# Five instruction lists of a fused attention and gated-MLP kernel, written anew

## The chip, the cores and the metric

The kernel runs on one core of a Trainium2 chip. The metric is the device time of one execution in microseconds. The core has five engines that each work through a list of instructions of their own, in order: TensorE (matmuls, here PE or "pe"), VectorE (DVE, "dve"), ScalarE (ACT, "act"), GpSimd (POOL, "pool") and SyncE (SP, "sp"), which here issues loads and stores. They meet at semaphores only. An instruction that waits holds up everything behind it on its engine.

## The reference

One block of a network on 2048 tokens of width 448: local attention with a residual, then a gated MLP that mixes over tokens, with a residual.

```python
# A: 16 heads of 28; a token attends to 8 keys, 2 apart, ending at itself
qkv = layernorm(x) @ wqkv                       # 448 -> 3 * 448
attn = softmax(where(mask, q . k[pos - 2*w] * 28**-0.5, -1e9))   # w = 0..7
h = x + (attn @ v) @ wo
# B: Fh = 896
z = gelu_tanh(layernorm(h) @ w_in)              # 448 -> 1792
z1, z2 = z[..., :896], layernorm(z[..., 896:])
g = w_sp @ z2 + b_sp[:, None]                   # 2048 x 2048 over tokens
h2 = h + (z1 * g) @ w_out                       # 896 -> 448
```

Inputs and output are bf16.

## The kernel before

The program is cut into 677 tasks. A task is a named piece of work, from one DMA to 56 TensorE instructions, with the tasks that it depends on and the buffers that it takes and gives back (`Task`, L196). Which engine runs which tasks, in which order, is written out in one constant: `SEQ` (L35) holds five tuples of task numbers, for SP, POOL, DVE, ACT and PE. `Planner.replay` (L300) goes through the five tuples, at each step issues the task that could start first by its table of costs, and picks buffers on the way: PSUM as pairs of its eight banks, two slots for exponentials (`E`), two for reciprocals (`L`), three for values (`V`), four for transposed tiles (`tr`), three for sums (`ub`). Copies, some small functions and some DMAs may run on either of two engines (`alts`); the tuple in which the number stands decides. Its costs include one for TensorE's instructions: blocks of `CHUNK, ASK, NEED = 256, 118, 434` (L243), read as 256 instructions a block, asked for at instruction 118 and needed at 434 of the count. ScalarE's functions lie in two tables, one with exp and ln, one with gelu; a load (L508) is put in wherever the list goes from one to the other.

The tokens are cut into 16 blocks of 128. Block u and block u + 8 form unit u (0 to 7); units are worked from 7 down to 0. The names, with the lines that record them:

- `x*` (L553), `w*` (L566), `wo*` (L936), `win*` (L588): loads. `wsp0_b` and `wsp1_b` (L946) load block b of the mixing matrix transposed, lower and upper half; each waits for the one before it. `w_out` (L1044) may go when all attention is over, and `wsp1_7`, first of its half, waits on SP until w_out has landed.
- `bn1`, `rs1`, `nrm1` and `bn2`, `rs2`, `nrm2` (L656, L657, L646, L676): the first and second layernorm. The result is transposed into `xh` by TensorE and a copy (`tT`, L692; `ev1`, L641 on ScalarE, L643 on VectorE) or by a DMA from SP (`tD`, L683).
- `cp*` (L641, L643): copies of the weights into the layout of the matmuls (k, q, v; `cpw` for w_in).
- `mmk`, `mmq` (L783), `mmv` (L823) with the copies `evk`, `evq`, `evv` (L641, L643): the projections, in four chunks of the tokens.
- Nine attention tiles i of 114 tokens of each half: `mml` (L858) logits, `exp` (L870), `mask` (L877), `mmr` (L886) row sums, `ln` (L899), `rex` (L921), `mmo` (L911) weighted values, `ot` (L929) their product with the reciprocal.
- `mmy` (L964) and `h` (L972): output projection and residual of a unit; mmy of a unit needs all tiles that reach it.
- `mmz2` (L984), `ge` (L994), `bn3` (L1000), `ag3`, `rs3`, `nrm3` (L1014): second half of the MLP's first product ("second MLP product"), its gelu and layernorm. `mmz1` (L1028), `gz1` (L1038): the first half.
- `g` (L1064): mixing over tokens, with `ua`, `um` (L1073, L1081). `wo` (L1093), `oa` (L1103), `st` (L1108): last product, residual, store.

Each engine's tasks carry waits only where a dependency crosses engines. A wait for an earlier DMA that a task carries is a wait of the engine that issues it. The waits, the buffers and the order of the engines are thus all consequences of `SEQ`.

Of the kernel before, what the change touches and what calls it, by code (L numbers as in the profile page):

```python
# [35 lines left out]
    (5, 1, 4, 8, 11, 19, 13, 3, 12, 16, 300, 306, 10, 15, 17, 18, 297, 302, 14, 21, 296, 58, 20, 299, 76, 298, 70, 82, 64,  # L36
     310, 301, 311, 312, 307, 313, 314, 315, 305, 316, 333, 387, 369, 317, 351, 318, 319, 423, 405, 320, 498, 321, 441, 322,
     459, 500, 323, 501, 502, 324, 503, 325, 504, 505, 506, 507, 508, 499, 509, 510, 511, 512, 513, 514, 515, 596, 593, 626,
     566, 632, 629, 569, 563, 599, 602, 560, 635, 660, 664, 668, 672, 676),
    (28, 31, 26, 24, 29, 27, 25, 55, 87, 48, 85, 73, 86, 330, 384, 366, 348, 402, 420, 438, 341, 456, 395, 359, 413, 467,  # L40
     431, 377, 449),
    (23, 30, 40, 32, 33, 39, 35, 93, 36, 42, 94, 43, 38, 100, 54, 90, 91, 53, 88, 47, 99, 46, 56, 71, 57, 96, 49, 78, 50, 72,
     52, 65, 74, 75, 66, 77, 59, 68, 80, 69, 60, 81, 121, 62, 168, 63, 151, 125, 142, 176, 159, 303, 131, 139, 304, 83, 202,
     185, 210, 327, 193, 329, 328, 219, 345, 347, 236, 331, 227, 363, 332, 253, 381, 244, 382, 383, 364, 270, 385, 399, 386,
     261, 365, 287, 346, 367, 368, 417, 418, 278, 349, 295, 350, 401, 400, 309, 435, 419, 436, 421, 422, 403, 453, 455, 437,
     404, 454, 336, 339, 390, 375, 439, 440, 340, 393, 357, 457, 458, 394, 429, 372, 408, 354, 342, 426, 411, 376, 462, 465,
     412, 466, 358, 447, 444, 360, 430, 361, 396, 448, 343, 433, 378, 414, 397, 469, 468, 415, 451, 379, 432, 450, 583, 584,
     556, 574, 575, 580, 577, 557, 581, 571, 550, 572, 578, 586, 551, 589, 547, 590, 587, 553, 613, 614, 554, 607, 643, 608,
     604, 644, 548, 524, 622, 605, 619, 620, 534, 525, 595, 544, 535, 616, 545, 623, 592, 617, 610, 649, 611, 640, 625, 650,
# [1114 lines left out]
```

## Time and profile before

| | us |
|---|---|
| median of three runs (lowest, highest) | 242.42 (241.69, 245.83) |
| profiled execution | 242.73 |
| its span from first to last instruction | 240.9 |
| TensorE busy | 233.1 |
| VectorE busy | 140.3 |
| ScalarE busy | 96.1 |
| GpSimd busy | 26.9 |

Three stages can be told apart in the trace. Up to about 9.7 us loads and the first normalisation; then projections, attention, and the MLP's first product, in which three engines work side by side; from 120.5 us on the mixing product and the last product, in which VectorE adds and multiplies and stores leave at the end. Rows of the chain read: start, microseconds, what. Rows of the waits read: who waited, for whom, microseconds in total, times, longest. "issue" means that nothing in the profile shows what was waited for. In the groups: line, engine, operation, shapes, count, busy microseconds, mean nanoseconds of one, idle time before it.

### The profile page before, as it was taken

The page shows a single profiled execution, that of the slowest core. Times are in us where ns is not written, and L with a number is a line of the kernel's source. Part 1 is how long each engine was busy: PE and PEld are TensorE (multiplying, and loading weights), DVE is VectorE, ACT ScalarE, POOL GpSimd, SP SyncE. Part 2 cuts the span into 40 slices and gives each one's busy share as a digit, 9 for nine tenths or more (in the row PEclk, how much of TensorE's full clock was granted, in tenths as well). Part 3 has the DMA queues.
Part 4 walks back from the last instruction along what each step waited for, and adds up shares of the span by engine and source line. Part 5 has one row for each costly group of instructions (what it writes and reads, how often), then busy time and mean ns, then how long its engine had stood idle before and what let it go on. Part 6 is the DMA issues. An engine that isn't in the chain of part 4 may idle for free.

```text
span 240.9 us, 6695 instructions
## 1 busy us (share of the span) xinstructions
PE 233.1 (97%) x3009; PEld 119.9 (50%) x3019; DVE 140.3 (58%) x280; ACT 96.1 (40%) x113; POOL 26.9 (11%) x66
## 2 busy tenths in 40 slices
PE   7898999999999999999999999999999999999995
PEld 2486865456554544554444444444444444444453
DVE  5999959378999899788810050253101436554443
ACT  2996988889899947764730000000000000000000
POOL 4062000002014321304600000000000000000000
PEclk9999999999999999999999999999999999999999
DMA  7949575574213557987632733350000000010122
GB/s 213 337 106 103 112 125 95 97 127 53 44 22 77 109 85 174 169 133 117 141 76 58 174 68 65 85 46 0 0 0 3 0 0 19 20 60 0 38 93 78
DMA packets 54628, 20.01 MB, mean 83 GB/s; under 512 B 46792, under 2 KB 54472, under 8 KB 54600
## 3 DMA queue, kind: packets, MB, share of 16 engines
q1 hardware_dynamic: 53496, 18.67, 39.6%
q10 hardware_dynamic: 1104, 0.92, 1.3%
q8 instruction: 23, 0.38, 0.7%
q14 instruction: 5, 0.04, 0.1%
HBM read 6.37 MB, written 1.84 MB: 34 GB/s over the span
## 4 chain that ended last, share of the span: by engine, by line
PE 88%; DVE 5%; DMA 2%; issue 1%; POOL 1%; ACT 1%; SPq 0%
PE psum L1064 40%; PE psum L783 11%; PE psum L1093 9%; PE psum L984 8%; PE psum L964 5%; PE psum L823 5%; PE psum L1028 4%; PE psum L858 2%; PE psum L911 2%; DMA x_tm<-in_A_x_dram 2%; DVE z2p L1014 2%; PE psum L886 1%; DVE st L1000 1%; DVE tring L676 1%; POOL rs L647 1%
## 5 line engine op out<-in xcount | busy, mean ns | idle before, releaser
L1073 DVE TENSOR_TENSOR ub<-psum,reg 128x512 bf16<-128x512 f32 x28 | 18.9, 687 | 68.7 <-PE psum L1064 66.4
L1064 PE MATMUL psum<-reg,z2p 128*128 128x512 bf16 x220 | 49.4, 379 | 0.2
L1064 PE MATMUL psum<-wspT_lo,z2p 128*128 128x512 bf16 x218 | 48.5, 379 | 0.4 <-DVE z2p L1014 0.2
L1064 PEld LDWEIGHTS psum<-wspT_lo,z2p 128*128 128x128 bf16 x224 | 21.8, 98 | 26.6 <-issue 0.4
L1064 PEld LDWEIGHTS psum<-reg,z2p 128*128 128x128 bf16 x224 | 21.9, 98 | 26.2
L783 PE MATMUL psum<-xh,reg 64*128 64x128 bf16 (+2 forms) x448 | 26.0, 270 | 0.2
L1093 PE MATMUL psum<-reg 128*128 128x448 bf16 (+2 forms) x119 | 22.2, 341 | 0.1
L984 PE MATMUL psum<-w_in,xh 64*128 64x448 bf16 x224 | 22.2, 349 | 0.0
L1028 PE MATMUL psum<-xh,w_in 64*128 64x512 bf16 x196 | 21.8, 376 | 0.0
L641 ACT ACTIVATE reg<-psum 128x896 bf16<-128x896 f32 (+2 forms) x25 | 20.0, 844 | 1.9 <-PE psum L783 1.0
L783 PEld LDWEIGHTS psum<-xh,reg 64*128 64x128 bf16 x448 | 16.8, 94 | 7.8 <-issue 0.8
L656 DVE BATCH_NORM_STATS2 st<-x_tm 128x6 f32<-128x448 bf16 x32 | 19.6, 612 | 1.4 <-DMA x_tm<-in_A_x_dram 1.2
L1000 DVE BATCH_NORM_STATS2 st<-z2p 128x6 f32<-128x448 bf16 x32 | 17.5, 611 | 3.1 <-ACT z2p L994 3.1
L870 ACT ACTIVATE reg<-psum 128x928 bf16<-128x928 f32 x18 | 16.2, 939 | 4.1 <-PE psum L858 4.1
L646 POOL TENSOR_SCALAR rs<-mv 128x2 f32<-128x2 f32 x19 | 7.5, 393 | 88.4 <-DVE mv L657 70.2
L1038 ACT ACTIVATE reg<-psum 128x1024 bf16<-128x1024 f32 x14 | 13.6, 1029 | 8.0 <-PE psum L1028 8.0
L1093 PEld LDWEIGHTS psum<-reg 128*128 128x128 bf16 x119 | 11.4, 98 | 10.4
L994 ACT ACTIVATE z2p<-psum 128x896 bf16<-128x896 f32 x16 | 14.2, 916 | 5.6 <-PE psum L984 5.6
L1103 DVE TENSOR_TENSOR tring<-psum,x_tm 128x448 bf16<-128x448 f32 (+2 forms) x17 | 10.1, 596 | 10.2 <-PE psum L1093 10.1
L984 PEld LDWEIGHTS psum<-w_in,xh 64*128 64x128 bf16 x224 | 10.6, 94 | 10.4 <-issue 0.4
L929 DVE TENSOR_TENSOR reg<-psum,reg 128x912 bf16<-128x912 f32 x9 | 11.1, 1235 | 7.2 <-ACT reg L921 6.6
L1028 PEld LDWEIGHTS psum<-xh,w_in 64*128 64x128 bf16 x196 | 9.5, 94 | 11.5
(63 smaller groups left out, 205.9 us busy)
## 6 DMA issues: line engine op xcount, KB each, us to landing
x_tm<-in_A_x_dram SPq DMA_DIRECT2D x15, 112.0 KB, 4.2
out_dram<-tring SPq DMA_DIRECT2D x15, 112.0 KB, 1.7
w_in<-in_B_w_in_dram SPq DMA_DIRECT2D x2, 448.0 KB, 4.5
reg<-in_B_w_out_dram SPq DMA_DIRECT2D x1, 784.0 KB, 6.0
z2p<-in_A_wqkv_dram ACTq DMA_DIRECT2D x2, 336.0 KB, 4.5
reg<-in_B_b_sp_dram SPq DMA_DIRECT2D x1, 512.0 KB, 4.6
w_in<-in_B_w_in_dram SPq DMA_DIRECT2D x2, 224.0 KB, 4.3
reg<-in_A_wo_dram SPq DMA_DIRECT2D x4, 98.0 KB
```

What stands on the lines that cost most here:

```text
L641: iss("act", lambda e: e.activation(dst, src, AF.Copy), reads=rd, writes=wr)
L656: iss("dve", lambda e: e.bn_stats(st[:, b, :], x_tm[:, b, :]), reads=[r_x[b]], writes=[rl[b]])
L783: iss("pe", lambda e, c=c, s=s, gi=gi, lhs=lhs: e.matmul(psum[:, bk[s] * 512 + cw * gi:bk[s] * 512 + cw * gi + cw], lhs, xh[64 * s:64 * s ...
L870: iss("act", lambda e: e.activation(E[:, es[0], 2 * n:2 * n + 2, :], pair_view(lb, 0, 8 * JW), AF.Exp, scale=SCALE), reads=[r_bank[lb[0]], ...
L984: iss("pe", lambda e, k2=k2, c=BLK[s][k2], s=s: e.matmul(psum[:, zb[s] * 512:zb[s] * 512 + D], xh[64 * s:64 * s + 64, c, HX + 128 * u:HX + ...
L994: iss("act", lambda e: e.activation(z2p[:, u:u + 9:8, D * k:D * k + D], pair_view(zb, 0, D), AF.Gelu_apprx_tanh), reads=[r_bank[zb[0]], r_ ...
L1000: iss("dve", lambda e, b=b: e.bn_stats(st3[:, b, k, :], z2p[:, b, D * k:D * k + D]), reads=[r_z2[b][k]], writes=[r_st3[b][k]])
L1028: iss("pe", lambda e, k=k, c=BLK[s][k], s=s: e.matmul(psum[:, bk[s] * 512:bk[s] * 512 + 512], w_in[64 * s:64 * s + 64, k, 128 * f:128 * f ...
L1038: iss("act", lambda e: e.activation(z1p[f].rearrange("p (s t) -> p s t", s=2)[:, :, 512 * ch:512 * ch + 512], pair_view(bk, 0, 512), AF.Ge ...
L1064: iss("pe", lambda e, b=b: e.matmul(psum[:, gb[0] * 512:gb[0] * 512 + 512], z2p[:, b, 128 * f:128 * f + 128], src[:, b, 512 * (tc % 2):512 ...
L1073: iss("dve", lambda e: e.tensor_tensor(ub[:, us_[0], :], psum[:, gb[0] * 512:gb[0] * 512 + 512], bb[:, 512 * tc:512 * tc + 512], ALU.add), ...
L1093: iss("pe", lambda e, f=f: e.matmul(psum[:, wb[0] * 512 + d0:wb[0] * 512 + d1], z1p[f][:, 128 * m:128 * m + 128], w_out[:, f, d0:d1], star ...
```

## The change

Only `SEQ` changes: about 560 of the 677 positions hold another number. No task is added, taken away or resized, so TensorE has the same matmuls, and the table of costs stays.

- PE: the first projection is mmk3_2 (before: mmq3_0). mmv2, mmv1, mmv0 come later. The second MLP products of units 7 and 6 move up, to between the small products of tiles 4 to 2: "mmz2_7_0 mml2 mmy4 mmo3_0 mmo3_1 mmz2_7_1 mmz2_6_1 mmz2_6_0 mmo3_2 mmr2 mmo3_3 mmv1" (before, unit 7's stood among tiles 1 and 0, unit 6's behind all attention). The end of the attention reads "mmz2_5_1 mmr0 mmo0 mmo1 mmz2_5_0 mmz2_4_1 mmy0 mmy1 mmz2_4_0". The first groups of the mixing product stand in another order; from the thirteenth on all is as it was.
- ACT: "exp2_0 exp2_1 ge7_0 ge7_1 ge6_1 ge6_0 ln2 rex2 exp1_1 exp1_0 exp0_0 exp0_1 ln1 rex1 ln0 rex0 ge5_0" (before: "... exp0_0 exp0_1 ge7_1 rex1 ln0 rex0 ge7_0 ..."). gz1_1_0 comes last.
- Between DVE and ACT, work changes hands. To DVE: cpk001, cpq000, cpv1, cpw0_0, evk0_1, evk0_3, evk1_0, evv0, evv1. To ACT: cpk010, cpq001, cpq010, ev1_5, ev1_7, evk0_2, evk1_2, evq0_2, evq1_2. From ACT to POOL: rs1_0, rs1_3; the other way: rs1_1.
- DVE: cpw1_0, cpw0_1 and cpw0_0 stand between tiles 6 and 3, bn3_7_1 before ot2; the normalisations of units 7, 6 and 5 come earlier.
- SP: weights change queues (wq0, wq1, wv1 to SP; wk1, wv0 to ACT) and loads their order. In the second half: "wsp0_11 tD2_3 w_out wsp0_2 tD2_0 wsp1_7 tD2_2 tD2_1 wsp0_10" (before: "tD2_2 tD2_3 wsp0_2 w_out wsp0_10 tD2_1 wsp0_1 tD2_0 wsp1_7"). The last store, st15_1, leaves from ACT's queue.

The parts of the diff that hold the above, with the numbers (251 exp2_0, 335 ge7_0, 338 ge7_1, 356 ge6_1, 353 ge6_0, 255 ln2; 498 w_out, 500 wsp1_7, 423 tD2_2, 441 tD2_1, 459 tD2_0; 334, 337 mmz2_7, 355, 352 mmz2_6):

```diff
-    (5, 1, 4, 8, 11, 19, 13, 3, 12, 16, 300, 306, 10, 15, 17, 18, 297, 302, 14, 21, 296, 58, 20, 299, 76, 298, 70, 82, 64,
-     310, 301, 311, 312, 307, 313, 314, 315, 305, 316, 333, 387, 369, 317, 351, 318, 319, 423, 405, 320, 498, 321, 441, 322,
-     459, 500, 323, 501, 502, 324, 503, 325, 504, 505, 506, 507, 508, 499, 509, 510, 511, 512, 513, 514, 515, 596, 593, 626,
...
+    (4, 1, 5, 9, 6, 7, 11, 10, 12, 306, 19, 16, 302, 15, 17, 13, 21, 300, 18, 20, 297, 58, 296, 14, 76, 82, 70, 64, 298, 299,
+     301, 310, 311, 305, 312, 307, 313, 333, 314, 351, 315, 369, 316, 387, 317, 318, 319, 405, 498, 320, 459, 500, 423, 441,
+     321, 501, 322, 502, 323, 324, 503, 325, 504, 505, 506, 507, 499, 508, 509, 510, 511, 512, 513, 514, 515, 596, 593, 626,
...
-    (0, 6, 7, 9, 22, 2, 34, 95, 41, 92, 101, 45, 97, 89, 144, 107, 161, 115, 98, 105, 113, 103, 111, 109, 117, 166, 178, 67,
...
-     137, 133, 192, 217, 218, 212, 235, 234, 221, 226, 229, 251, 252, 238, 243, 255, 260, 268, 269, 263, 280, 272, 285, 286,
-     338, 277, 289, 294, 335, 389, 308, 371, 392, 374, 356, 353, 497, 485, 493, 491, 495, 410, 428, 407, 489, 425, 443, 461,
...
+    (0, 3, 2, 8, 22, 34, 41, 90, 38, 45, 98, 97, 105, 94, 103, 111, 93, 144, 95, 113, 161, 109, 52, 73, 107, 115, 117, 150,
...
+     187, 192, 137, 212, 234, 218, 217, 235, 246, 221, 226, 238, 229, 243, 251, 252, 335, 338, 356, 353, 255, 260, 269, 268,
+     285, 286, 272, 277, 289, 294, 371, 374, 389, 489, 392, 497, 410, 491, 487, 407, 464, 495, 461, 425, 428, 443, 475, 446,
...
-    (84, 37, 44, 106, 143, 160, 114, 104, 112, 110, 102, 108, 116, 51, 145, 146, 162, 147, 148, 163, 177, 122, 120, 164, 165,
...
-     266, 267, 262, 398, 271, 256, 257, 258, 259, 281, 282, 283, 284, 337, 416, 273, 274, 288, 275, 276, 334, 388, 290, 291,
-     292, 293, 434, 452, 373, 370, 391, 484, 352, 355, 496, 494, 492, 490, 409, 427, 406, 424, 488, 445, 442, 460, 463, 482,
...
+    (84, 37, 44, 104, 102, 110, 112, 143, 160, 51, 108, 106, 116, 114, 177, 145, 146, 147, 148, 124, 122, 118, 162, 163, 164,
...
+     181, 182, 326, 203, 138, 134, 186, 205, 188, 189, 190, 206, 207, 208, 191, 136, 211, 230, 231, 344, 213, 214, 215, 216,
+     245, 232, 233, 362, 220, 228, 237, 222, 223, 224, 225, 334, 247, 248, 249, 250, 380, 239, 240, 337, 355, 352, 241, 254,
+     242, 262, 256, 257, 258, 259, 264, 265, 266, 267, 398, 279, 281, 282, 283, 284, 416, 271, 373, 288, 290, 291, 292, 273,
+     274, 293, 275, 276, 370, 391, 452, 434, 388, 488, 494, 496, 409, 406, 490, 486, 463, 460, 427, 484, 424, 442, 445, 474,
...
```

34 rows, old and new, of the table SEQ are left out of this document.

## The prediction

> **What bounds the kernel now.** I read the page's busy times and its slices first.
>
> ```profile
> PE 233.1 (97%) x3009; PEld 119.9 (50%) x3019; DVE 140.3 (58%) x280; ACT 96.1 (40%) x113; POOL 26.9 (11%) x66
> PE   7898999999999999999999999999999999999995
> DVE  5999959378999899788810050253101436554443
> ACT  2996988889899947764730000000000000000000
> PEclk9999999999999999999999999999999999999999
> ```
>
> TensorE is busy in every slice after the start and has its full clock. VectorE and ScalarE come close to it only until about 120 us; in the second half (the token-mixing product and the output product) they mostly wait. A busy TensorE need not be a fast one, so next come its waits (microseconds, times, longest) behind the first product, and the chain in order of time (start, microseconds).
>
> ```profile
> PE psum L858 <- issue: 0.9, 1, 0.9
> PE psum L964 <- DVE mv L657: 0.8, 1, 0.8
> PE psum L823 <- issue: 0.3, 1, 0.3
> PE psum L1064 <- DVE z2p L1014: 0.2, 1, 0.2
> ```
>
> ```profile
> 5.92 0.64 DVE st L656
> ...
> 9.66 0.96 PE psum L783 x28
> ...
> 20.16 0.87 issue
> ...
> 52.35 0.26 issue
> ...
> 72.35 0.50 issue
> ...
> 120.50 10.72 PE psum L1064 x49
> ...
> 238.37 0.31 DVE tring L1103
> ```
>
> From 9.66 us, the first projection, to 238.3 us, the end of the last product, TensorE stands still for 0.9 + 0.8 + 0.3 + 0.2 = 2.2 us. The change reorders work and removes no matmul, so everything behind the start can yield 2.2 us at most. Of 242.42 us, 2% are 4.85 us, about what a measurement of this kernel can tell from no change. A gain of that size would need another 2.6 us from the 9.66 us of the start, where the first normalisation waits for loads until 5.92 us. So faster by over 2% is nearly excluded; the question is how much waiting the new order adds.
>
> **The change, part by part.** The sum is made against the profiled execution, 242.73 us (span 240.9), which lies 0.3 us above the median of the three runs, 242.42. I keep that distance.
>
> *The start.* The first product is now that of k, no longer of q. Rows of ScalarE's and VectorE's timelines (start, microseconds):
>
> ```profile
> 7.34 0.21 ACT L669 ACTIVATE rs<-rs 128x2 f32<-128x2 f32 x1
> 8.41 1.70 ACT L641 ACTIVATE reg<-reg 64x1792 bf16<-64x1792 bf16 x1
> 10.13 0.92 ACT L641 ACTIVATE xh<-psum 128x896 bf16<-128x896 bf16 x1
> 6.58 0.18 DVE L657 BATCH_NORM_AGGREGATE mv<-st 128x2 f32<-128x6 f32 x1
> 6.68 0.36 DVE L676 TENSOR_SCALAR tring<-x_tm,mv,rs 128x448 bf16<-128x448 bf16 x1
> 9.55 0.51 DVE L643 COPY reg<-reg 64x1344 bf16<-64x1344 bf16 x1
> 13.20 0.58 DVE L643 COPY reg<-z2p 64x1792 bf16<-64x1792 bf16 x1
> ```
>
> Four x tiles still come first, in another order, so the statistics end as now, at 6.76. On VectorE follow four normalisations and three k copies: 4 x 0.36 + 2 x 0.51 + 0.58 = 3.0, or 9.8 with gaps. On ScalarE stand the second unit's rstd (0.5, from 6.76), cpk010 (1.70, the row of that shape) and ev1_7, which moves there (0.92): 6.76 + 0.5 + 1.70 + 0.92 = 9.9. TensorE starts at about 10.05 in place of 9.66: **+0.4**. Bounds: -0.2 (VectorE as now) and +1.0 (the k weights, now issued first, land one copy later). Nothing hides this, since each later matmul waits behind the first. The weights that change between SP's and ScalarE's queues cost nothing further: ScalarE issues fewer of them ahead of its table load, and SP's next x load waits for x7 and x15 to land in either order.
>
> *TensorE's pauses.* Three of the rows above name no releaser.
>
> ```profile
> q8 instruction: 23, 0.38, 0.7%
> ```
>
> That queue carries 0.38 MB in 23 packets, 16.5 KB each; over the 6028 TensorE instructions of the page that is one packet per 262 instructions. The kernel's planner holds that a block of 256 is asked for at 118 and needed at 434 (CHUNK, ASK, NEED). Counted down the old list, two instructions a matmul, the pauses at 20.16, 52.35 and 72.1 stand at instructions 696, 2480 and 3756; 434 plus 1, 8 and 13 blocks is 690, 2482 and 3762. So I take them for late blocks. They come where the 316 instructions between asking and needing last only 4.5, 5.2 and 4.5 us by the rows; a stretch of 4.6 us had no pause. In the new list all stretches up to the attention's last tiles last 5.4 us or more, since value and second-MLP products stand between the small matmuls; three in a row late in the attention (before mml1_00, mml0_10 and mmo1_0) last 4.6, 4.3 and 4.65. So 0.87 + 0.26 + 0.75 = 1.9 go and I put back 1.2 for those three: **-0.7**. Bounds: -1.9 (none pauses) and +0.7 (all three pause by 0.87).
>
> [...]
>
> *Second MLP product and GELU among the exponentials.*
>
> ```profile
> L994 ACT ACTIVATE z2p<-psum 128x896 bf16<-128x896 f32 x16 | 14.2, 916 | 5.6 <-PE psum L984 5.6
> L508 ACT ACT_TABLE_LOAD x4 | 5.1, 1283 | 3.0 <-issue 2.9
> 96.14 5.30 PE psum L984 x56
> 30.83 2.77 PE psum L823 x56
> 34.47 3.13 PE psum L783 x28
> 78.72 3.13 PE psum L964 x16
> 78.80 1.23 DVE L929 TENSOR_TENSOR reg<-psum,reg 128x912 bf16<-128x912 f32 x1 [0.55 <-PE psum L911]
> L972 DVE TENSOR_TENSOR x_tm<-psum,x_tm 128x896 bf16<-128x896 f32 x8 | 8.7, 1086 | 2.5 <-PE psum L964 2.4
> L643 DVE COPY w_in<-w_in 64x3584 bf16<-64x3584 bf16 (+1 forms) x3 | 3.3, 1087 | 0.1
> L1000 DVE BATCH_NORM_STATS2 st<-z2p 128x6 f32<-128x448 bf16 x32 | 17.5, 611 | 3.1 <-ACT z2p L994 3.1
> ```
>
> Old and new both load tables four times. In the old order one gelu lies between two loads inside the attention (1.28 + 0.92 + 1.28 = 3.5), in the new one four (6.2). Behind them wait ln2, rex2, the last two tiles' exponentials, and so on VectorE ot2, ot1, ot0. Does TensorE feel it? The test is mmy0, which needs ot0. Today ot0 ends at 80.03 and the second product of the 78.72 row starts near 80.3: 0.2 us to spare. Between mmy7 and mmy0 the new list puts five second-MLP products (5 x 1.33), mmv2 (1.39), the last three q products (3 x 1.57) and mmr5, mmr6, mmo5 (1.2), and drops mmz2_4_0 and mmy1 (2.9): 13.9 - 2.9 = 11.0 us more. ScalarE between rex6 and rex0 gets three gelus (2.75), evv2 and evq0_1 (1.9) and loses evv1 and evv0 (1.8): 2.8 more. VectorE between h7 and ot0 gets three w_in copies (3.3), two value copies (2 x 1.09, by L972's size), ot5 (1.23), a pair of L1000 (1.2) and one normalisation (0.36): 8.2 more. So both keep their place, VectorE with 0.2 + 11.0 - 8.2 = 3.0 us to spare. The products of units 7 and 6 also want their transposed tiles sooner (unit 6 by 20.3 us of TensorE's list), and VectorE's list has moved the normalisations before them up by about as much (19.6), so those tiles keep their lead. What is left are single waits for a PSUM pair: mmz2_7_1 must wait until exp2_1 has freed one, mmr0 for its mask behind evv0, mmo1_0 for h2. I take **+0.6**; bounds 0 and +2.7 (the three gelus in full).
>
> *Before the mixing product.* Eight first-MLP products still follow the last second product, nrm3 has the same length, and the 0.2 before L1064 may go: **-0.15**, bounds -0.2 and +1.0 (the new third entry, g0_6_0, wants all of nrm3 0.4 us sooner). From there on the lists differ only in small swaps.
>
> *The last store.*
>
> ```profile
> 233.71 5.54 SPq L1108 DMA_DIRECT2D out_dram<-tring  x6
> ```
>
> SP issues stores until 239.25; the last sum, begun at 238.37, ends at 238.68. From ScalarE's empty queue the last store need not wait for the issue of the one before it: **-0.15**, bounds -0.4 and +0.1.
>
> Sum: 0.4 - 0.7 + 0.6 - 0.15 - 0.15 = 0.0. The profiled execution stays at 242.7, a median at **242.4 us**. [...]
>
> **The rivals.** *Slower: a load at the head of SP's queue.*
>
> ```profile
> 86.81 1.08 DVE L972 TENSOR_TENSOR x_tm<-psum,x_tm 128x896 bf16<-128x896 f32 x1
> 92.43 0.58 SPq L1044 DMA_DIRECT2D reg<-in_B_w_out_dram  x1
> 103.38 1.30 SPq L946 DMA_TRANSPOSE reg<-in_B_w_sp_dram  x1
> reg<-in_B_w_out_dram SPq DMA_DIRECT2D x1, 784.0 KB, 6.0
> DMA to landing us min/median/max: 2.9/3.0/6.2
> ```
>
> Now wsp1_7, which waits on SP until w_out has landed, is issued at 103.38, behind every transpose of unit tiles (L683). In the new list tD2_2 and tD2_1 stand behind it. w_out may go after the last h, now at 87.9 and by the list 1.6 later: 89.5. It lands 6.0 later, wsp1_7 takes 1.3, tD2_2 lands 2.9 to 6.2 after that (transposes into xh): 99.7 to 103.0. TensorE wants it for mmz2_2_1 near 101.4, the end of the four groups of the 96.14 row, which have as much matmul work before them. So 0 to 1.6 us are lost: within the forecast. But each further microsecond of w_out is one of the end. If it needs 11 us or more while transposes share the engines, the stall passes 5 us: **248 us**. Against it: 6.0 was measured with transposes around it. Chance 0.10. [...]
>
> *ScalarE becomes the bound of the attention's end.* Its slices there read 8 and 9; if the 3.0 us to spare are not there, the three gelus cost all of 2.7 in place of 0.6: 242.4 + 2.1 = 244.5. Chance 0.17.
>
> *All pauses go.* The three dense stretches pass, too, and the PSUM waits are nothing: 242.4 - 1.2 - 0.6 = 240.6. Chance 0.15.
>
> *Pauses do not follow the order:* they came from the transfers of the moment, the same 1.9 us stay, and 242.4 + 0.7 = 243.1. For it speaks that a block lands by DMA beside others, against it that all three stand at a block's end. Chance 0.08.
>
> **How the numbers follow.** The forecast has 0.50. Its own range, with half of the bounds, is 240.9 to 244.5. The range for 8 in 10 leaves out the slow rival and the far ends of the bounds: 242.4 - 2.2 = 240.2 (the start 0.6 below what I took, the pauses 1.2, the PSUM waits 0.4) and 242.4 + 3.9 = 246.3 (gelus +2.1, w_out's 1.6, 0.2 of the tail). Slower by over 2% (247.3): the slow rival's 0.10 and 0.02 for the gelus and the queue together, 0.12. Faster by over 2% (237.6): 0.02, for a start I misjudge. Within: 0.86.
>
> **What would show it.** First projection near 10.05 us. No pause over 0.2 us without a releaser before 65 us, up to three between 66 and 80 us. A ScalarE stretch of load, four gelus, load of 6.2 us, with TensorE's waits beside it below 1 us. tD2_2 issued right after wsp1_7 near 97 us. L1064 starting between 119.5 and 121.5, then 118 us to the end as now. The prediction is wrong if TensorE waits several microseconds for PSUM or VectorE between 60 and 100 us, or at mmz2_2_1.

## The result and the profile after

| | before | after |
|---|---|---|
| median, us (20 runs each) | 242.43 | 243.86 |
| lowest and highest | 241.23, 245.83 | 242.76, 245.59 |
| profiled execution | 242.73 | 242.96 |
| its span | 240.9 | 241.2 |

The ratio is 1.0067, with a 95% interval of 1.0045 to 1.009: the new order is slower by 0.7%, or by 1.4 us of the medians. The forecast was no change at 242.4, with a range of 240.2 to 246.3. The time lies in the range, but the forecast is missed by more than the measurement is uncertain.

The two profiled executions differ by 0.23 us only, so most of the difference is not in this trace. First, what is in it. These are TensorE's waits in the changed kernel (microseconds, times, longest), all of them:

```profile
PE psum L692 <- DVE tring L676: 2.1, 2, 1.1
PE psum L635 <- DVE warm L614: 1.5, 1, 1.5
PE psum L984 <- DVE x_tm L972: 0.5, 1, 0.5
PE psum L783 <- ACT reg L641: 0.5, 2, 0.3
PE psum L858 <- ACT reg L899: 0.3, 1, 0.3
```

No pause without a releaser is left: the old list had 0.9 and 0.3 of them and a third inside a wait of 0.8. New are the waits for the addition of L972, for the copies of L641 and for the logarithm of L899. The first row was, in the kernel before:

```profile
PE psum L692 <- DVE tring L676: 1.0, 2, 0.6
```

TensorE now stands idle for twice as long around the first two transposes. Its timeline there (start, busy, what, idle time before it) and VectorE's:

```profile
2.76 4.28 PE L635 MATMUL psum<-warm 128*128 128x512 bf16 x12
8.11 0.56 PE L692 MATMUL psum<-ident,tring 128*128 128x128 bf16 x7 [1.07 <-DVE tring L676]
9.69 0.56 PE L692 MATMUL psum<-ident,tring 128*128 128x128 bf16 x7 [1.02 <-DVE tring L676]
10.22 3.30 PE L783 MATMUL psum<-xh,reg 64*128 64x128 bf16 x112
```

```profile
6.79 0.85 DVE L643 COPY reg<-z2p 64x1344 bf16<-64x1344 bf16 x1
...
8.37 0.85 DVE L643 COPY reg<-z2p 64x1344 bf16<-64x1344 bf16 x1
```

The first projection starts at 10.32 us by the chain (rows of matmuls overlap a little, hence the 10.22) instead of 9.66. The two copies (cpk001 and cpk011) stand between the normalisations that the transposes wait for, at 0.85 us each. Before, two smaller copies stood there:

```profile
7.06 0.39 DVE L643 COPY reg<-z2p 64x672 bf16<-64x672 bf16 x1
8.18 0.39 DVE L643 COPY reg<-z2p 64x896 bf16<-64x896 bf16 x1
```

That is 2 x 0.46 = 0.92 us more. The last statistics ended 0.27 us sooner than in the trace of before (6.49 instead of 6.76), because their x tile had landed sooner, which leaves the 0.65 us.

From the first projection to the first mixing product, and from there to the last residual, busy times by engine (window, its length, busy time and instructions of PE, PEld, DVE, ACT and POOL, granted clock, two DMA figures), after and before:

```profile
10.32:120.74 110.42, 108.97 (x2423) 61.33 (x2422) 93.91 (x189) 86.90 (x102) 25.63 (x53) 1.00 0.62 110
120.74:238.85 118.11, 118.07 (x569) 55.15 (x567) 40.90 (x74) 1.94 (x2) 0.00 (x0) 1.00 0.18 43
```

```profile
9.66:120.49 110.83, 108.64 (x2424) 61.98 (x2426) 94.12 (x189) 89.12 (x105) 24.12 (x51) 1.00 0.62 111
120.49:238.37 117.88, 117.37 (x557) 55.02 (x565) 38.76 (x75) 1.82 (x2) 0.00 (x0) 1.00 0.19 43
```

The middle stage is shorter by 0.41 us: TensorE's idle time fell from 110.83 - 108.64 = 2.2 to 1.45, and its busy time grew by 0.3. The last stage is longer by 0.23. So this execution reads +0.66 at the start, -0.41, +0.23 and -0.2 at the last store: +0.3 of span.

What the trace doesn't show is in the list of executions. Of the 20 of the changed kernel, 9 have a mean granted clock of 0.986 to 0.993 and a median of 244.65 us; the other 11 have 0.999 or 1.0 and a median of 243.21. So the runs at a lower clock are 1.4 us longer. A stretch of 3.41 us at half clock, as e4_new_start's trace below has one (9.74 to 13.15 us, mean clock 0.993), lowers the mean by 0.007 and costs, as an estimate from its length, up to half of it, 1.7 us. Of the 106 executions of the kernel before that ran beside the experiments, 2 are below 0.999.

### The profile page after: what moved, and what is told of

It is laid out like the page before. It is cut to its first block, busy times and chain, and to the rows that moved or that the text cites. A ratio compares the mean times of both kernels' runs of the same rounds, so it can differ in the third digit from the quotient of the medians.

```text
span 241.2 us, 6695 instructions
## 1 busy us (share of the span) xinstructions
PE 233.8 (97%) x3019; PEld 119.3 (49%) x3019; DVE 143.2 (59%) x280; ACT 93.8 (39%) x111; POOL 28.4 (12%) x68
## 4 chain that ended last, share of the span: by engine, by line
PE 86%; ACT 5%; DVE 4%; DMA 1%; POOL 1%; issue 1%
PE psum L1064 40%; PE psum L783 9%; PE psum L1093 9%; PE psum L1028 9%; PE psum L984 9%; PE psum L964 5%; ACT reg L641 3%; PE psum L823 2%; PE psum L858 2%; DVE st L656 1%; ACT reg L899 1%; DMA x_tm<-in_A_x_dram 1%; PE psum L911 1%; DVE tring L676 1%; DVE x_tm L972 1%
## 5 line engine op out<-in xcount | busy, mean ns | idle before, releaser
L1064 PE MATMUL psum<-wspT_lo,z2p 128*128 128x512 bf16 x224 | 49.0, 379 | 0.0
L641 ACT ACTIVATE reg<-psum 128x1024 bf16<-128x1024 f32 (+2 forms) x24 | 19.3, 844 | 2.3 <-PE psum L783 1.9
L647 POOL TENSOR_TENSOR rs<-rs,nhalf 128x2 f32<-128x2 f32 x20 | 16.8, 842 | 1.7
L646 POOL TENSOR_SCALAR rs<-mv 128x2 f32<-128x2 f32 x20 | 6.4, 318 | 87.3 <-DVE mv L657 72.9
```

The costliest lines, as they stand in the source:

```text
L641: iss("act", lambda e: e.activation(dst, src, AF.Copy), reads=rd, writes=wr)
L647: iss("pool", lambda e: e.tensor_tensor(dst, dst, nh, ALU.pow), reads=rr + [r_nhalf], writes=rr)
L1064: iss("pe", lambda e, b=b: e.matmul(psum[:, gb[0] * 512:gb[0] * 512 + 512], z2p[:, b, 128 * f:128 * f + 128], src[:, b, 512 * (tc % 2):512 ...
```

## The experiments

Edits are given in the names of the tasks; "DVE", "PE" and so on are the tuples of SEQ. In the experiments' profiles the line numbers are higher by one or two. Ratios are to the kernel before, with 95% intervals.

**The start and the rest, put together crosswise.** In e3_old_start the new lists follow the old lists' start; in e4_new_start the old lists follow the new start.

```diff
 e3_old_start
-SP, POOL, DVE, ACT, PE: new lists
+SP up to x0, POOL to c_kpad, DVE to nrm1_13, ACT to evq2_2, PE to tT1_5: old lists
+then what is left of the new lists, in their order
 e4_new_start
-SP, POOL, DVE, ACT, PE: old lists
+SP up to x3, POOL to c_ones, DVE to cpq100, ACT to ev1_5, PE to mmq2_0: new lists
+then what is left of the old lists, in their order
```

> The new lists behind the old lists' start (loads, first normalisation of units 7 to 4, copies of the q, k and v weights, first projections up to the transpose of unit 5, with mmv6 behind tile 8's logits as before). Start theory: the first projection at 9.7 us, clock as in the kernel before, and the pauses that went stay gone: 241.3 to 242.2 us, at or below the kernel before. Attention theory: 243.5 to 244 us.

> The old lists behind the new lists' start, the mirror of the run before. Start theory: first projection at 10.3 us, a clock below 1.0 in part of the executions, and the old pauses: 243.3 to 244.3 us. Attention theory: as the kernel before, 242.4 us.

Measured: e3_old_start 245.2 (ratio 1.0094, 1.0061 to 1.0127), e4_new_start 245.6 (1.0124, 1.0086 to 1.0163). Both missed. A row of e3_old_start's timeline of TensorE (in brackets the idle time):

```profile
50.52 0.28 PE L912 MATMUL psum<-reg 64*32 64x58 bf16 x23 [1.35 <-issue]
```

Its first projection started at 9.67, as in the kernel before, but a pause of 1.35 us without a releaser came back, and at the seam TensorE waited three times for ScalarE (0.49, 0.35 and 0.46). These 2.65 us, less the 0.5 that the changed kernel waits for L641 and the 0.64 won at the start, give 1.5 of the 2.2 us by which its profile (245.18) lies above the changed kernel's. So each crossing makes waits of its own, and neither run prices the start. One part of what was expected came true: e4_new_start, which has the new start and otherwise the old lists, had the clock at 0.993 in four of six runs, its profile too. e3_old_start had it below 1.0 in two of six; in its profile TensorE stood idle for 2.0 us around the first two transposes, though the lists there are the old ones.

**The pauses.** e5_blocks and e12_shift leave every list as it is and put more, smaller warm-up products (fill) ahead of everything, which moves the ends of TensorE's instruction blocks as the planner counts them.

```diff
 e5_blocks
-for _ in range(n): matmul(psum[512 columns], warm[:, 0:128], warm[:, :])
+for _ in range(4 * n): matmul(psum[128 columns], warm[:, 0:128], warm[:, 0:128])
 e12_shift
-fill("f0", 15), each 512 columns
+fill("f0", 55), the first 11 of 512 columns, 44 of 64
```

> The new lists; only the 15 warm-up matmuls of 512 columns are 60 of 128, the same columns in all. That adds 90 TensorE instructions at the front, so that every block of 256 ends 90 instructions earlier in the work. If the pauses are late blocks, pauses without a releaser come back where 316 instructions now last 2.8 and 2.9 us by the old rows (near the logits and values of tiles 5 to 7, and at the end of the attention) and smaller ones at 4 us: 3 to 6 us in all, 246 to 250 us. If they come from the transfers of the moment: no more than 0.5 us beside the new lists.

> The lists of the changed kernel; the 15 warm-up products become 11 and 44 narrow ones of 64 columns, which take about as long together, so that 80 more instructions of TensorE lie ahead of everything and all ends of its instruction blocks of 256 move by 80. Block theory: by the changed kernel's own durations the stretches between asking and needing shrink to 2.9 us at two places (near 43 and near 84 us) and to 4.0 at two more, so pauses with nothing to wait for come back, one of 1 to 2 us at 43, and 2 to 5 us in all: a profile of 245 to 248. If pauses don't follow where the blocks end, 243 to 244 as the changed kernel.

Measured: e5_blocks 250.03 (one execution), e12_shift 249.06 (1.0266, 1.0227 to 1.0306), profile 248.48. Both profiles lie just above the ranges expected. e12_shift's pauses:

```profile
34.53 0.35 PE L888 MATMUL psum<-reg,ones 64*32 64x464 bf16 x1 [0.59 <-issue]
...
45.63 0.26 PE L860 MATMUL psum<-reg 32*64 32x58 bf16 x8 [1.10 <-issue]
...
87.76 2.24 PE L986 MATMUL psum<-w_in,xh 64*128 64x448 bf16 x21 [1.78 <-issue]
```

They come at the two places that the count gave (43 and 84, here 44.5 and 86, since the first projection was 1.1 us later and the earlier pauses lie ahead), and at a third: 3.5 us in all. Counted down the list, two instructions a matmul, they fall in the tasks in which instructions 1458, 1970 and 4274 stand (mmr7, mml6_11, mmz2_5_0), which are the planner's 434 plus 4, 6 and 15 of its blocks of 256. With the same work in the same order, e5_blocks paused in the last two of these by 1.15 at 47 and 2.08 at 89. So these pauses move with the number of instructions ahead of them, and stand where the planner's blocks are needed; that they are late blocks is the author's reading of this. e5_blocks also shows another cost: VectorE's cpk001 stood 1.96 us for its weights, and the first transposes, whose normalisation is queued behind it, came at 10.14 instead of 8.11. Both kernels had a half-speed stretch at the start (mean clock 0.993), so their times hold up to 1.7 us of that beside the pauses.

**The clock.** e9_before_short is the kernel before with less warm-up, e1_fills and e13_gap_fills the changed kernel with more.

```diff
 e9_before_short
-fill("f0", 15), each 512 columns
+fill("f0", 15), the first 10 of 512 columns, 5 of 64
 e1_fills
-fill("f0", 15)
+fill("f0", 18)
+fill("f1", 4), in PE: f0 tT1_7 f1 tT1_6
 e13_gap_fills
+fill("f1", 3), in PE: f0 tT1_7 f1 tT1_6
```

> The kernel before, with the last 5 of the 15 warm-up products at the start 64 columns wide instead of 512: as many instructions, every list as it was, but TensorE stands idle before the first transpose for about 1.5 to 2.0 us instead of 0.47. Clock theory: with that much idle time in the start, a third or more of the runs show a granted clock of 0.993 or less and are 1.2 to 1.8 us longer than the others, median 243.0 to 244.0. If gaps at the start don't drop the clock: 1.0 in all runs and 242.2 to 242.7.

> The new lists with more warm-up matmuls: 18 in place of 15 at the start, and 4 between the first two transposes, where TensorE stood idle for 1.07 and 1.02 us (before: 0.47 and 0.56). Start theory (the idle spells shut the clock gate for a stretch in some executions): a granted clock of 1.0 in nearly all executions and a median 0.7 to 1.2 us below the new lists, 242.7 to 243.2 us; the first projection still at 10.3 us. Attention theory (the clock and the time go in waits between 50 and 100 us): nothing changes, 243.9 us.

> The changed kernel with one addition: three warm-up products between its first two transposes, where TensorE stands idle for 1.02 us. They take 0.65 us at full clock, so nothing behind them moves; TensorE's idle time between 7 and 10 us goes from 2.1 to about 1.45 us. Clock theory: a window of 3.41 us that is less than half busy no longer comes about, the clock is 1.0 in at least ten of twelve runs, and the median falls from 243.86 to 242.9 to 243.3, where the changed kernel's runs without a half-speed stretch lie. If the half-speed stretches don't come from these gaps, the median stays at 243.6 to 244.1 with 0.993 in a third or more.

Measured: e9_before_short 243.71 (1.0057, 1.0036 to 1.0079), with 0.993 in 7 of 12 runs; e1_fills 243.82 (1.0061, 1.0032 to 1.009), 0.995 in one of 9 and 1.0 in the rest; e13_gap_fills 243.29 (1.006, 1.0037 to 1.0083), 1.0 in 12 of 12.

e9_before_short has the old lists to the last number, and less warm-up alone, with the longer gap behind it, made it as slow as the changed kernel. The 23 executions of the kernel before beside it all had 1.0. Its 0.993 runs lie around 243.6, not above the others as expected, and its profiled execution says why one can't go by the mean clock alone. TensorE's timeline, mean granted clock 1.0:

```profile
7.50 0.93 PE L693 MATMUL psum<-ident,tring 128*128 128x128 bf16 x7 [1.28 <-DVE tring L677]
8.83 0.93 PE L693 MATMUL psum<-ident,tring 128*128 128x128 bf16 x7 [0.40 <-DVE tring L677]
9.69 1.50 PE L784 MATMUL psum<-xh,reg 64*128 64x128 bf16 x28
```

The transposes take 0.93 instead of 0.56 and the projection 1.50 instead of 0.96. At a granted clock of 0.50 e12_shift's second transpose took 0.93, too (at 10.55 us), but here slices of 1 us from 7.5 to 10.5 us read 1.00: the clock had not yet risen, and time before the rise does not count into the mean. So this run has two causes in it, stretches at half speed behind the rise and a late rise, and doesn't part them. e13_gap_fills closes one of the changed kernel's two gaps and moves nothing behind it; its timeline:

```profile
8.41 0.81 PE L636 MATMUL psum<-warm 128*128 128x512 bf16 x3
9.60 0.57 PE L693 MATMUL psum<-ident,tring 128*128 128x128 bf16 x7 [0.37 <-DVE tring L677]
```

With it the half-speed stretches went from 9 of 20 runs to none of 12. The median fell by 0.57 us, to where the changed kernel's runs without a stretch lie, as expected. Beside it the kernel before was at 242.27, so the distance to it fell by 0.4 only, from 1.43 to 1.02, and the ratio fell less still, from 1.0067 to 1.006, with intervals that overlap. So that the gaps bring the stretches is shown; their share of the difference, 0.4 to 0.6 us by the medians, is not shown as clearly, and the changed kernel itself was not run again on that chip. e1_fills removed the stretches as well, one run at 0.995 apart, but its 18 products ended at 7.9 where 15 ended at 7.04 and its median did not fall: expected 242.7 to 243.2, missed.

What a gap has to be like is seen in windows of 3.41 us, the length of a half-speed stretch: slices of 1 us of e4_new_start from 9.5 to 13.5 us read 0.62, 0.50, 0.50 and 0.67, so its stretch lasted from 9.74 to 13.16. The windows are counted in whole steps from the moment at which the clock rose; in the changed kernel's trace this is 5.84 us, where the warm-up products go from 634 ns each to 379 (window, length, PE busy; last but two the clock). Changed kernel, kernel before, e5_blocks, e4_new_start, e12_shift and e7_mlp_back, which is told below:

```profile
5.84:9.25 3.41, 1.77 (x13) 0.74 (x11) 3.32 (x8) 3.01 (x6) 0.00 (x0) 1.00 1.11 329
```

```profile
6.67:10.08 3.41, 2.33 (x34) 1.40 (x34) 3.29 (x9) 3.34 (x5) 0.00 (x0) 1.00 1.07 329
```

```profile
5.01:8.42 3.41, 1.67 (x29) 1.50 (x27) 1.70 (x5) 1.01 (x4) 0.00 (x0) 1.00 1.08 325
8.42:11.83 3.41, 0.68 (x9) 0.51 (x10) 2.96 (x6) 2.61 (x2) 0.00 (x0) 1.00 1.08 305
```

```profile
6.33:9.74 3.41, 1.52 (x12) 0.59 (x9) 3.32 (x8) 2.90 (x4) 0.00 (x0) 1.00 1.10 341
9.74:13.15 3.41, 3.22 (x53) 3.02 (x55) 3.30 (x8) 2.44 (x4) 0.00 (x0) 0.50 1.10 323
```

```profile
6.84:10.25 3.41, 1.66 (x43) 1.36 (x40) 2.74 (x6) 2.82 (x4) 0.00 (x0) 1.00 1.10 339
10.25:13.66 3.41, 3.11 (x51) 2.92 (x53) 3.30 (x8) 2.35 (x4) 0.00 (x0) 0.50 1.11 322
```

```profile
59.88:63.29 3.41, 1.69 (x138) 1.31 (x123) 3.34 (x6) 3.41 (x5) 0.00 (x0) 1.00 0.45 89
63.29:66.70 3.41, 3.32 (x56) 1.35 (x54) 1.00 (x3) 1.24 (x2) 0.93 (x2) 0.50 0.71 60
66.71:70.12 3.41, 0.00 (x0) 0.00 (x0) 3.31 (x7) 0.00 (x0) 1.14 (x2) 1.00 0.00 0
70.12:73.53 3.41, 3.35 (x52) 1.44 (x52) 2.60 (x4) 1.92 (x2) 0.70 (x1) 0.50 0.02 5
```

TensorE was busy for 1.77 (52%) and 2.33 us (68%) in the first two, and the clock stayed. It was busy for 0.68 (20%), 1.52 (45%), 1.66 (49%), 1.69 (50%) and 0 us in the others, and the next window ran at half clock (e5_blocks' from 11.84 on). One window doesn't fit a sharp boundary: with 1.67 us (49%) e5_blocks kept its clock at 8.42. So in these traces the boundary lies at about half, and the changed kernel's profiled execution escaped by a hair. Where the windows lie changes from trace to trace: at the starts shown they are counted from 5.84, 6.67, 5.01, 6.33 and 6.84 us.

**The start by itself.** e6_pool_copy takes one k copy out of VectorE's list. e10_pool_fills and e14_pool_17 add warm-up to it.

```diff
 e6_pool_copy
-DVE ... nrm1_6 cpk011 nrm1_14 cpk000 ...
+DVE ... nrm1_6 nrm1_14 cpk000 ...
-POOL ... c_wkp rs1_5 ...
+POOL ... c_wkp cpk011 rs1_5 ...
 e10_pool_fills: the same, and
-fill("f0", 15)
+fill("f0", 21)
 e14_pool_17: the same, and
-fill("f0", 15)
+fill("f0", 17)
```

> One of the four copies of the K weights (cpk011) goes from VectorE's list to GpSimd's, behind c_wkp; TensorE's list is untouched, so its instruction blocks end where they ended. Start theory: without the 0.85 us of cpk011 ahead of it nrm1_14 ends at about 8.8, the second transpose starts at 8.9 instead of 9.69, its idle time goes from 1.02 to about 0.2, and the first projection starts at about 9.8 (ScalarE's copy of the first transpose ends at 9.72 in the changed kernel) instead of 10.3: a profile of 242.3 to 242.7, clock 1.0 in all or all but one of the runs, and a median of 242.4 to 243.0. If the half-speed stretches have nothing to do with TensorE's gaps at the start, about half of the runs still show 0.993 and the median stays at 243.4 to 243.9. If GpSimd's copy is slow (over 3 us), the first projection waits for it and the time is above 244.

> As e6_pool_copy, with 21 warm-up products instead of 15, which end at about 8.0 us instead of 6.5, so that TensorE stands idle before the first transpose for about 0.3 us instead of 1.83. Clock theory: no half-speed stretch after the clock has risen, the runs of e6_pool_copy at 243.6 to 245.9 go, 242.3 to 242.8 in nearly all runs, median 242.3 to 242.7: the time of the kernel before within 0.3%. If the idle time is not the cause, a quarter of the runs stay above 243.5 as with e6_pool_copy.

> As e6_pool_copy with 17 warm-up products instead of 15 (21 in e10_pool_fills made the transposes themselves late, 8.73 instead of 8.34). Here they end at about 7.0 to 7.5, ahead of the transposes. Start theory and clock theory together: the first projection at about 10.0 as in e6_pool_copy, 0.993 in at most one of twelve runs, a median of 242.3 to 242.8. If the remaining difference to the kernel before is not at the start, 242.8 to 243.3 with the clock at 1.0.

Measured: e6_pool_copy 242.94 (1.0044, 1.0017 to 1.0072), profile 242.51, 0.993 in 3 of 12; e10_pool_fills 243.6 (1.0056, 1.0034 to 1.0079); e14_pool_17 242.71 (1.0034, 1.0002 to 1.0067), 1.0 in all. TensorE's timeline of e6_pool_copy, and GpSimd's:

```profile
8.34 1.18 PE L693 MATMUL psum<-ident,tring 128*128 128x128 bf16 x14 [1.83 <-DVE tring L677]
10.02 3.30 PE L784 MATMUL psum<-xh,reg 64*128 64x128 bf16 x112 [0.51 <-issue]
```

```profile
6.80 1.34 POOL L644 COPY reg<-z2p 64x1344 bf16<-64x1344 bf16 x1 [2.88 <-DMA z2p<-in_A_wqkv_dram]
```

The second transpose now follows the first at once, the first projection starts at 10.02 (expected 9.8), 0.1 us behind ScalarE's copy of the first transpose, and the profile is 0.45 below the changed kernel's, as expected. Why this gain lasts to the end can be read from the chain of the changed kernel. ScalarE's copies run without a gap from its copy of the second transpose to this place:

```profile
17.89 0.61 ACT reg L641
...
18.54 2.54 PE psum L783 x84
```

TensorE waited 0.35 us for the copy that ends at 18.50. From 18.54 to the start of the last residual, at 238.85, it is 220.3 us. In e6_pool_copy the same two moments are 18.07 and 238.38, in e14_pool_17 18.49 and 238.80, in e15_norm_first 19.09 and 239.50, in e16_loads_later 17.74 and 238.17: 220.3 or 220.4 us in each. So in these profiles, with no stretch at half speed and no pause at the end of a block, the time goes with the moment at which ScalarE is done with its copies, and a later start is paid in full, through ScalarE.

The price of e6_pool_copy is a longer gap ahead of the transposes (1.83 us), hence the stretches in 3 runs, where one at most was expected. With 21 warm-up products these were all but gone (0.993 in one run of 12, 0.997 in another), but the products themselves lasted to about 8.7 and held the transposes up, and the median missed the 242.3 to 242.7 expected. With 17 the products were out of the way and the clock stayed, but the profiled start was no earlier: VectorE stood 0.69 us for weights and the first projection came at 10.45 (expected 10.0). Of the changed kernel's excess two thirds were gone by the medians (1.43 to 0.44 us above the kernel before), half by the ratios (1.0067 to 1.0034). The interval's lower end touches the kernel before. One of the 12 runs took 1350.04 us, which nothing on record explains; the interval leaves it out, and without it the median is 242.56.

Three more of e14_pool_17's runs were still at 244.5 to 245.5 with the clock at 1.0. e11_two_pool, e15_norm_first and e16_loads_later went after these and after a version that beats both kernels.

```diff
 e11_two_pool: as e6_pool_copy, and
-DVE cpk001; ACT ev1_7
+POOL c_wkp cpk011 cpk001; DVE nrm1_14 ev1_7
+fill("f0", 18); fill("f1", 3), in PE: f0 tT1_7 tT1_6 f1
 e15_norm_first: as e14_pool_17, and
-DVE nrm1_7 cpk001 nrm1_15
+DVE nrm1_7 nrm1_15 cpk001
 e16_loads_later: as e15_norm_first, and
-SP x6 x15 x14 wv1 wq0 wq1 x13 x5 x4
+SP x6 x15 x14 wv1 x13 x5 wq0 x4 wq1
```

> Two of the four copies of the K weights (cpk011, cpk001) go to GpSimd, VectorE evicts the first transpose (ev1_7) instead of ScalarE, 18 warm-up products instead of 15 and 3 more between the second transpose and the first projection. Start theory: the transposes start at about 7.5 and 8.2, the first projection at about 9.55 (GpSimd's second copy ends there, at 1.34 each from 6.8) instead of 10.3: a profile of 241.8 to 242.3, clock 1.0, median 241.8 to 242.4, at least as fast as the kernel before. If what is gained at the start is lost again by the end of the attention, 242.4 to 243.0.

> As e14_pool_17, and VectorE's remaining copy of K weights ahead of the transposes (cpk001) goes behind nrm1_15, so that the first transpose hangs on no load of weights. That load landed 4.6 to 7.0 us after its issue in the profiled runs (4.8 in the changed kernel, 5.5 in e14_pool_17, where VectorE stood 0.69 us for it with the second half of the first tile's normalisation queued behind). Load theory: the first transpose starts at 7.5 to 7.9 in every run, the first projection at about 9.8, the runs of e14_pool_17 at 244.5 to 245.5 get fewer (one of twelve or none), median 242.1 to 242.5. If late loads are not what makes those runs long, still a quarter of them above 244.

> As e15_norm_first, and on the sync queue the two loads of the Q weights, 336 KB each by pieces, go behind the x tiles 13, 5 and 4, out of the way of the K weights' loads. Load theory: the K weights land at most 5 us after their issue, no wait of VectorE, GpSimd or ScalarE for them, no run above 244, median 241.9 to 242.4; the copies of the Q weights come later in VectorE's list and still find them there. If the Q weights then come too late, a wait at the Q projections (17 to 21 us) of 0.5 to 2 us and 243 to 244.5.

Measured: 243.5 (1.0062, 1.0033 to 1.0091), 243.44 (1.002, 0.9994 to 1.0046) and 243.02 (1.003, 1.0005 to 1.0055). None beats the kernel before. In e11_two_pool the expectation failed on VectorE: its normalisations, found by their tile (count, shortest/median/longest in ns), beside GpSimd's two copies:

```profile
L677 DVE TENSOR_SCALAR tring<-x_tm,mv,rs x4: 365/835/1443, 6.3 to 8.2; 128x448 bf16<-128x448 bf16 x4
```

```profile
6.67 2.81 POOL L644 COPY reg<-z2p 64x1344 bf16<-64x1344 bf16 x2 [2.74 <-DMA z2p<-in_A_wqkv_dram]
```

Two of the four took 1.28 and 1.44 us instead of 0.39, while GpSimd copied from 6.67 to 9.48, and the last of them ended at 9.61, so the first projection came at 10.82 instead of 9.55. The copy of 0.85 us that VectorE ran beside GpSimd's in e6_pool_copy (7.00 to 7.85, GpSimd's 6.80 to 8.14) was not slowed. Why the one is slowed and the other not, no run shows. The late projection is not what makes this profile long, 244.54: ScalarE, which had one copy less, was done as early as in the changed kernel, and the last residual started at 238.85 in both. What was late were the last stores (KB, median us from issue to landing; e11_two_pool, then the changed kernel):

```profile
out_dram<-tring ACTq DMA_DIRECT2D x1, 36.0 KB, 3.2
```

```profile
out_dram<-tring ACTq DMA_DIRECT2D x1, 36.0 KB, 1.6
```

Here 1.6 us of a long run at full clock are thus the landing of the last stores. The profiled execution of e15_norm_first met a slow normalisation, too (two of them together 1.66 us, 0.67 in e16_loads_later's): a first projection at 10.76 and 243.93. In e16_loads_later's it was 9.70, with 242.52; one of its 12 runs was above 244, against three of 12 without its change, two of these with the clock at 0.993. So late weights are perhaps part of the long runs, beside late stores; the medians of e15_norm_first and e16_loads_later, above what was expected, don't show it. This stays open.

**The attention.** e7_mlp_back takes the second MLP products out from among the exponentials. e8_three_waits is e6_pool_copy with the two products that waited moved.

```diff
 e7_mlp_back
-PE ... mmo4_3 mmz2_7_0 mml2 mmy4 mmo3_0 mmo3_1 mmz2_7_1 mmz2_6_1 mmz2_6_0 mmo3_2 ... mmr1 mmz2_5_1 mmr0 ... mmo1_3 mmz2_5_0
+PE ... mmo4_3 mml2 mmy4 mmo3_0 mmo3_1 mmo3_2 ... mmr1 mmr0 ... mmo1_3 mmz2_7_0 mmz2_7_1 mmz2_6_1 mmz2_6_0 mmz2_5_1 mmz2_5_0
-ACT exp2_1 ge7_0 ge7_1 ge6_1 ge6_0 ln2 ... rex0 ge5_0
+ACT exp2_1 ln2 ... rex0 ge7_0 ge7_1 ge6_1 ge6_0 ge5_0
-DVE nrm2_13 bn3_7_1 ot2 ... nrm2_10 bn3_7_0
+DVE nrm2_13 ot2 ... nrm2_10 bn3_7_1 bn3_7_0
 e8_three_waits
-PE mmz2_7_0 mml2_00 mml2_01 mml2_10 mml2_11 ... mml1_00 mml1_01 mml1_10 mml1_11 mmy3
+PE mml2_00 mml2_01 mml2_10 mml2_11 mmz2_7_0 ... mml1_00 mml1_01 mmy3 mml1_10 mml1_11
```

> The five products of the second MLP that the change put between the attention's products (both halves of units 7 and 6, one of unit 5) go back behind the last attention product, the GELUs of units 7 and 6 behind the last exponential, one statistics step of VectorE (bn3_7_1) with them. The prediction's step held that they cost 0.6 us where they are: the waits for the addition of L972 (0.5) and for the logarithm of L899 (0.3) go and nothing comes in their place: a profile of 242.0 to 242.6. Rival, that they are cover for TensorE while ScalarE works off the exponentials: without 7 us of products, waits of 1 to 4 us appear before the mixture products (L911) and the row sums (L886), and the profile is at 244 to 247.

> As e6_pool_copy, and two products change places on TensorE alone: the first half of unit 7's second MLP product goes behind the four score products of tile 2, and the output product of tile 3 goes ahead of the second half of tile 1's scores. If the waits of 0.5 us (for the addition of L972) and 0.3 us (for the logarithm of L899) were on the path that sets the end, 0.6 to 0.8 us below e6_pool_copy: a profile of 241.5 to 242.1, and faster than the kernel before. If the same banks are then waited for by the products that moved ahead, the same time as e6_pool_copy within 0.3 us.

Measured: e7_mlp_back 252.05 (1.0402, 1.0375 to 1.0429), profile 251.22; e8_three_waits 245.28 (1.0104, 1.0065 to 1.0142), profile 243.39. TensorE's waits in e7_mlp_back:

```profile
PE psum L887 <- DVE reg L878: 4.4, 2, 3.6
...
PE psum L965 <- DVE reg L930: 1.3, 1, 1.3
```

Both expectations were too low. Without the products TensorE waited for masks (L878) and for the products with the reciprocal (ot, L930) that VectorE hadn't got to, and two windows fell to half clock, the one at 63.29 above and the one behind the empty window. All its waits together are 5.5 us more than the changed kernel's, and two windows at half clock cost up to 3.4; its profile is 8.3 us longer. So in the new order the five products are cover, and dear to do without. This doesn't price them against the old order, which has other work there. In e8_three_waits the waits moved:

```profile
PE psum L824 <- DVE reg L930: 0.6, 1, 0.6
...
PE psum L859 <- DVE x_tm L973: 0.4, 1, 0.4
...
PE psum L965 <- ACT reg L900: 0.3, 1, 0.3
PE psum L985 <- ACT reg L642: 0.3, 1, 0.3
```

In place of 0.8 us there are 1.6, and its profile is 0.9 above that of e6_pool_copy, where 0.3 at most was expected. Each of the four is a wait for an engine that empties PSUM, so the waits went over to what stands next. Three of its six runs were below clock 1.0, so the median of 245.28 holds half-speed stretches, too.

## Why the prediction was right and wrong

- *The start, +0.4.* Right in sign, too small: +0.66, and not by the path that set the sum. There ScalarE's copy of the first transpose was last, at 9.9; it ended at 9.72, and the second transpose, behind both copies of VectorE, at 10.27. The failed term is these two copies, taken at 0.51 us from a row that is a copy of the V weights (cpv0, reg<-reg). They take 0.85. The trace of before had this price: cpk011 ran on VectorE there, hidden in a row of the timeline that lumps it with a larger copy, and the groups by form list it:

```profile
L643 DVE COPY reg<-z2p 64x1344 bf16<-64x1344 bf16 x1 | 0.9, 851 | 0.0
```

  Two times 0.34 is more than the 0.26 missing; that the x tile landed 0.27 sooner was luck. Once e6_pool_copy takes one copy away, the path by ScalarE is the last, at about 9.9.
- *The clock.* This is what the prediction missed most. It was no term of the sum, and the prediction never asked what the copies do to TensorE's idle time ahead of the first projection. Two gaps of 1.0 us around a product of 0.56 were enough in 9 of 20 executions, which are 1.4 us longer than the others. Windows that were 45 to 50% busy did it (1.52 to 1.69 of 3.41 us in e4_new_start, e12_shift and e7_mlp_back).
- *The pauses, -0.7.* Their places were right: e5_blocks and e12_shift moved them with the count of instructions, and e12_shift stood 3.5 us in them. The three dense stretches paused in no profiled execution of the changed kernel's lists, so -1.9 in the profile, the lower bound. That the kernel before loses all 1.9 in its usual execution is not shown: its profiled one lies 0.3 above its median.
- *Products and GELU among the exponentials, +0.6.* About right in size, 0.8: TensorE waited 0.5 us at the first of these products (mmz2_7_0, for L972) and 0.3 at a logits product of tile 1 (for L899), not at the three places that the prediction names. The ScalarE stretch came as described, 6.6 us, with a wait of 0.41 before the fourth gelu:

```profile
64.98 1.28 ACT L508 ACT_TABLE_LOAD   x1
66.27 2.68 ACT L994 ACTIVATE z2p<-psum 128x896 bf16<-128x896 f32 x3
69.36 0.92 ACT L994 ACTIVATE z2p<-psum 128x896 bf16<-128x896 f32 x1 [0.41 <-PE psum L984]
```

- *Before the mixing product, -0.15, and the last store, -0.15.* The wait for L1014 went, and the end came 0.2 sooner behind the last sum. From the mixing product on 118.1 us were needed instead of 117.9, which the sum had at nothing.
- *What else the sum had at nothing.* TensorE's two waits for ScalarE's copies in the projections (L641, 0.5 us; the last is the one at 18.54) and 0.3 us more busy time before the mixing product. "Nothing hides this" named the wrong reason: the late start counts because ScalarE is the bound up to 18.54.
- *The sum as a whole.* It had 0.0 and the profiled executions differ by 0.23, which is luck in part: the pauses gave 1.2 more than was taken, and the start (0.26), the waits among the exponentials (0.2), ScalarE's copies (0.5), the busy time (0.3) and the last stage (0.2) took it back. The range "with half of the bounds" would be 241.0 to 245.1 by the prediction's own bounds, not 240.9 to 244.5.
- *The rivals.* The load at the head of SP's queue stayed harmless: SP issued w_out at 89.91, wsp1_7 at 95.09 and tD2_2 at 96.30 (forecast near 97), and TensorE had no wait there.

```profile
95.09 1.17 SPq L946 DMA_TRANSPOSE reg<-in_B_w_sp_dram  x1
96.30 2.65 SPq L683 DMA_TRANSPOSE xh<-tring  x2
```

  ScalarE did not become the bound of the attention's end; it was the bound of the projections, which no rival had. All pauses went, but not to 240.6, since the waits stayed and the start cost more.

In sum, of 1.4 us the half-speed stretches are 0.4 to 0.6 by the medians (e13_gap_fills). Another 0.6 went with e14_pool_17 (1.02 to 0.44 us above the kernel before). Traces show that a late start is paid in full, but e14_pool_17's profiled start was not earlier than the changed kernel's, so that these 0.6 are the start is likely and not shown. What is left, 0.3 to 0.4, isn't settled: its interval nearly reaches zero, and part of it are long runs at full clock.

## What to carry to other kernels

A gap of TensorE had a second price here besides its length: of six windows of 3.41 us in which gaps left TensorE busy for 1.69 us or less, about half, five were followed by one at half speed. Two gaps of 1.0 us were enough in 9 of 20 executions. So look at how full such windows are, above all at the start, and look at the granted clock of many executions: the one trace of the changed kernel missed it by luck, at 1.77 us. When pieces of work move to another engine or place, take their durations from the row of the same piece, with shapes kept apart, since a timeline can lump it with another, and ask what is queued behind them. Ask, too, which engine has no gap behind the start: here it was ScalarE, up to 18.54 us in the changed kernel, and a later start was paid through it.

## What the runs showed of the hardware

- TensorE's clock halved after a window of 3.41 us in which it was busy for 1.69 us or less (five windows, from 0 to 1.69, in e4_new_start, e5_blocks, e7_mlp_back and e12_shift), and stayed after 1.77 us (changed kernel) and 2.33 (kernel before). In e5_blocks one with 1.67 us kept it, so in these traces the boundary lies at about half.
- The mean granted clock begins with the rise: an execution of mean 1.0 had transposes of 0.93 instead of 0.56 us, in slices that read 1.00 (e9_before_short).
- More warm-up was too much once: 21 products lasted to 8.7 us and held up the transposes (e10_pool_fills), 17 at about 7.5 did not (e14_pool_17).
- 80 instructions more ahead of unchanged lists cost three pauses of 0.59, 1.10 and 1.78 us further on (e12_shift).
- A VectorE normalisation of 0.39 us took 1.28 and 1.44 us beside two GpSimd copies (e11_two_pool), a VectorE copy of 0.85 beside one took its usual time (e6_pool_copy).
- The last store, 36 KB, landed 3.2 us after its issue in e11_two_pool and 1.6 in the changed kernel.
